# Loading the K and V caches of both batch entries as one unit of 4 MB

## The chip, the cores and the metric

One core of one Trainium2 chip runs the kernel; the other cores are idle. The metric is the device time of one execution in microseconds (us). PE is the matrix engine (TensorE), DVE is VectorE, ACT is ScalarE, POOL is GpSimd, and SyncE issues nearly all loads (77.66 of the 77.90 MB of packets are on its queue); a load writes into the 128 partitions (rows) of the on-chip memory. Ratios in this document are the mean time of one kernel's fast runs over that of the other's of the same rounds, so they are not quite the ratio of the medians that are quoted.

## The reference

It is one decoding step of attention over a cached window beside a dense layer, for two batch entries with one new token each:

```python
xn = layernorm(x)                                   # x is [2, 1, 448]
# A: 16 query heads, 8 key heads, Dh = 256; the last W = 4096 of 32768 cached positions
q = xn @ wq
p = softmax(q . k_cache[:, :, -4096:, :] / 16)
a = (p . v_cache[:, :, -4096:, :]) @ wo
# B: dense layer with a mish activation, 448 -> 1792 -> 448
h = xn @ w1 + b1
b = (h * tanh(softplus(h))) @ w2
out = x + a + b                                     # [2, 1, 448]
```

What matters is the amount of data: K and V are 2 entries x 8 heads x 4096 positions x 256 x 2 bytes each, 67.1 MB together. wq, wo, w1 and w2 add 10.6 MB. The compute is small.

The check of results is loose for this reference: softmax over 4096 nearly equal scores averages V to almost nothing, so the kernels below that mix up rows on purpose were also reported correct.

## The kernel before

Sixteen units (8 key heads x 2 entries), each with a 2 MB load of K and one of V. A load puts 32 positions (16 KB of contiguous memory) on each of the 128 partitions:

```python
def load_k(i):
    kvh, b = heads[i]
    t = k_pool.tile([P, T * Dh], BF16, tag="k", name="k")        # 4 buffers
    nc.sync.dma_start(
        out=t[:], in_=A_k_cache[b, kvh, s0:Sk, :].rearrange("(p t) d -> p (t d)", p=P)
    )
# load_v: the same from A_v_cache, 5 buffers; the last V comes in two halves
# load_wo: 448 KB for each key head
# ...
load_k(0); load_dense(); load_k(1)      # load_dense: w1 and w2
for i in range(NK + KA):
    # load_k(i + 2), load_v(i), load_wo
    # for each half: turn (DVE transposes K), scores (PE, ACT), turn_p (DVE transposes p)
    if i == 1:
        dense_out()                     # 28 products with w2
    if i >= KA:
        values(i - KA)                  # 64 products with V
        # mix: 8 products with wo, after every second unit
```

The softmax here doesn't subtract the row's maximum and nothing guards it: scores larger than these inputs give would overflow.

Of the kernel before, what the change touches and what calls it, by code (L numbers as in the profile page):

```python
# [9 lines left out]
ALU = mybir.AluOpType  # L10
AXIS = mybir.AxisListType
BF16 = mybir.dt.bfloat16
# [22 lines left out]
def kernel(  # L35
# [25 lines left out]
    F = B_w1.shape[1]  # L61
    T = W // P
    NH = 2
    TH = T // NH
    NX = 2
# [7 lines left out]
    NE = 2  # L73
    assert Sq == 1 and D * NX == NS * P and NS % 2 == 1 and HF % P == 0 and Hq % NX == 0
    assert TH * Q <= 512 and NB * NE * Q == Dh and ND == 2
# [3 lines left out]
    wo_pool = ctx.enter_context(tc.tile_pool(name="wo", bufs=3))  # L79
    k_pool = ctx.enter_context(tc.tile_pool(name="kk", bufs=4))  # L80
    v_pool = ctx.enter_context(tc.tile_pool(name="vv", bufs=5))
    kt_pool = ctx.enter_context(tc.tile_pool(name="kt", bufs=3))
# [14 lines left out]

    def v_tile(n):
        t = v_pool.tile([P, T * Dh], BF16, tag="v", name="v")
        return t[:, 0:n]  # L100



    SC = NS // 2 + 1
    wq_in = A_wq.rearrange("r (x n) -> (r x) n", x=NX).rearrange("(p s) n -> p s n", s=NS)
    wq_sb = []
    for lo, hi in ((0, SC), (SC, NS)):
        w = v_tile((hi - lo) * HW).rearrange("p (s n) -> p s n", n=HW)
        nc.sync.dma_start(out=w, in_=wq_in[:, lo:hi, :])  # L109
        wq_sb += [w[:, s, :] for s in range(hi - lo)]  # L110

# [35 lines left out]
    for b4 in range(NB):  # L147
        rows = slice(b4 * Q, (b4 + 1) * Q)
        for j in range(NQ):
            nc.vector.tensor_copy(  # L150
                out=spread[rows, b4, j * Q : (j + 1) * Q], in_=ident[rows, rows]
            )
    hsel = consts.tile([P, rep], FP32)
    nc.vector.tensor_copy(out=hsel[:], in_=ident[:, 0:rep])
    for j in range(1, NQ):
        nc.vector.tensor_tensor(
            out=hsel[:], in0=hsel[:], in1=ident[:, j * Q : j * Q + rep], op=ALU.add
        )
    NW = 3
    qdiag = []  # L160
# [46 lines left out]
    qrep = consts.tile([P, NB, HH, NE, NX, Bsz], BF16)  # L207
    wq_v = [w.rearrange("p (h m e) -> p h e m", h=HH, e=NE) for w in wq_sb]

    def project():  # L210
        qT_ps = ps_m.tile([P, HH, NE, NX * Bsz], FP32, tag="m", name="qT_ps")
        for hh in range(HH):
            for e in range(NE):
                for s in range(NS):
                    nc.tensor.matmul(  # L215
                        qT_ps[:, hh, e, :],
                        lhsT=wq_v[s][:, hh, e, :],
                        rhs=xs[:, s, :, :].rearrange("p x b -> p (x b)"),
                        start=(s == 0),
                        stop=(s == NS - 1),  # L220
                    )
# [11 lines left out]

    heads = [(kvh, b) for kvh in range(Hkv) for b in range(Bsz)]

    def build_q(i):
        kvh, b = heads[i]
        x, h0 = divmod(kvh * rep, HH)
        t = qdiag[i % NW]
        tv = t[:].rearrange("p (n e) c -> p n e c", e=NE)  # L240
        for j in range(NQ):
            rows = slice(j * Q, (j + 1) * Q)
            for e in range(NE):
                nc.gpsimd.tensor_copy(  # L244
                    out=tv[rows, :, e, j * Q : j * Q + rep],
                    in_=qrep[rows, :, h0 : h0 + rep, e, x, b],
                )
# [4 lines left out]

    def load_dense():
        dense["w1"] = v_tile(NS * HF).rearrange("p (s n) -> p s n", s=NS)
        nc.sync.dma_start(
            out=dense["w1"],
            in_=B_w1.rearrange("r (x n) -> (r x) n", x=NX).rearrange("(p s) n -> p s n", s=NS),
        )
        dense["w2"] = v_tile(NX * NF * D).rearrange("p (x c d) -> p x c d", x=NX, c=NF)
        nc.sync.dma_start(  # L260
            out=dense["w2"], in_=B_w2.rearrange("(x q c) d -> q x c d", x=NX, q=P)
        )

# [40 lines left out]
    def dense_out():  # L304
        w2_sb = dense.pop("w2")
        for x in range(NX):
            for c in range(NF):
                for n in range(NO):
                    add(
                        n,  # L310
                        act_bf[:, c, x, :],
                        w2_sb[:, x, c, n * DO : (n + 1) * DO],
                        start=False,
                        stop=False,
                    )


    NSTEP = len(heads) * NH
    k_t, kt_t, v_t, p_t, pT_t, wo_t = {}, {}, {}, {}, {}, {}
    state = {}  # L320

    def load_k(i):
        kvh, b = heads[i]
        t = k_pool.tile([P, T * Dh], BF16, tag="k", name="k")
        nc.sync.dma_start(  # L325
            out=t[:], in_=A_k_cache[b, kvh, s0:Sk, :].rearrange("(p t) d -> p (t d)", p=P)
        )
        k_t[i] = t

    def load_v(i, parts=1):  # L330
        kvh, b = heads[i]
        t = v_tile(T * Dh).rearrange("p (t d) -> p t d", t=T)
        vin = A_v_cache[b, kvh, s0:Sk, :].rearrange("(p t) d -> p t d", p=P)
        for u in range(parts):
            ts = slice(u * T // parts, (u + 1) * T // parts)
            nc.sync.dma_start(out=t[:, ts, :], in_=vin[:, ts, :])  # L336
        v_t[i] = t

    def load_wo(kvh, parts=1):
        w = wo_pool.tile([P, rep, ND * D], BF16, tag="wo", name="wo")  # L340
        r0 = kvh * rep * Dh
        win = A_wo[r0 : r0 + rep * Dh, :].rearrange("(h p c) d -> p h (c d)", h=rep, p=P)
        for u in range(parts):
            hs = slice(u * rep // parts, (u + 1) * rep // parts)
            nc.sync.dma_start(out=w[:, hs, :], in_=win[:, hs, :])
        wo_t[kvh] = w
# [11 lines left out]
    def scores(s):  # L358
# [13 lines left out]
        if s % NH == 0:  # L372
# [4 lines left out]
            func=ACT.Exp,  # L377
            scale=scale,
            accum_out=state["rs", i][:, s % NH : s % NH + 1],
        )  # L380
        p_t[s] = p_sb

    def turn_p(s):
        pT = p_pool.tile([P, TH * Q], BF16, tag="pT", name="pT", bufs=7)
        nc.vector.transpose(out=pT[:], in_=p_t.pop(s)[:])  # L385
# [4 lines left out]
        rs = state.pop(("rs", i))  # L390
        den = ps_den.tile([P, rep], FP32, tag="den", name="den")
        for n in range(NH):
            nc.tensor.matmul(  # L393
                den[:],
                lhsT=rs[:, n : n + 1].to_broadcast([P, P]),
                rhs=hsel[:],
                start=(n == 0),
                stop=(n == NH - 1),
            )
        state["rec", i] = small.tile([P, rep], FP32, tag="rec", name="rec", bufs=4)  # L400
        nc.vector.reciprocal(out=state["rec", i][:], in_=den[:])  # L401

    def values(i):
        kvh, b = heads[i]
        po = ps_o.tile([P, ND, rep], FP32, tag="o", name="o")
        vv = v_t.pop(i).rearrange("p t (m c) -> p t c m", c=ND)
        for t in range(T):
            half, th = divmod(t, TH)
            pTv = pT_t[i * NH + half][:].rearrange("p (t c) -> p t c", t=TH)
            for c in range(ND):  # L410
                nc.tensor.matmul(  # L411
                    po[:, c, :],
                    lhsT=vv[:, t, c, :],
                    rhs=pTv[:, th, 0:rep],
                    start=(t == 0 and c == 0),
                    stop=(t == T - 1),
                    skip_group_check=True,
                )
        if b == 0:
            state["oT"] = small.tile([P, ND, rep, Bsz], BF16, tag="oT", name="oT")  # L420
        oT = state["oT"]
        nc.vector.tensor_tensor(  # L422
            out=oT[:, :, :, b],
            in0=po[:],
            in1=state.pop(("rec", i))[:].unsqueeze(1).to_broadcast([P, ND, rep]),
            op=ALU.mult,
        )

    def mix(kvh):
        oT = state["oT"]  # L430
        w = wo_t.pop(kvh)
        for h in range(rep):
            for n in range(NO):
                for c in range(ND):
# [4 lines left out]
                        start=False,  # L439
                        stop=(kvh == Hkv - 1 and h == rep - 1 and c == ND - 1),  # L440
                    )

    NK = len(heads)
    KA = 2

    load_k(0)
    load_dense()
    load_k(1)
    project()
    build_q(0)  # L450
    build_q(1)
    turn(0)
    for i in range(NK + KA):
        if i + 2 < NK:
            load_k(i + 2)
        if i < NK:
            load_v(i, parts=1 if i < NK - 1 else 2)
            kvh, b = heads[i]
            if b == Bsz - 1:
                load_wo(kvh, parts=1 if i < NK - 1 else 2)  # L460
            for half in range(NH):
                s = i * NH + half
                if s + 1 < NSTEP:
                    turn(s + 1)
                scores(s)
                if s >= 1:
                    turn_p(s - 1)
            if i + 2 < NK:
                build_q(i + 2)
        if i == NK:  # L470
            turn_p(NSTEP - 1)
        if i == 0:
            dense_in()
        if i == 1:
            dense_out()
        if i >= KA:
            values(i - KA)
            kvh, b = heads[i - KA]
            if b == Bsz - 1:
                mix(kvh)  # L480

# [35 lines left out]
```

## Time and profile before

| | kernel before |
|---|---|
| median time | 194.66 us (194.61 to 194.78, 4 runs) |
| span in the profile | 192.7 us |
| read | 77.67 MB, mean 403 GB/s |
| PE busy, DVE busy | 130.4 us, 102.2 us |
| a 16 KB packet of K or V | mean 620 ns, median 613 ns |

The prediction shows the page's lines. To read them: the DMA row gives the mean busy share of the core's sixteen DMA engines in tenths, in 40 equal slices of the span. A 9 in nearly all slices says that the sixteen are full, so time is bytes over rate (77.67 MB at 403 GB/s are the 192.7 us of the span). In the trace each packet is one run of contiguous bytes, or one completion mark of a load: the 7652 packets on the SyncE queue of the kernel before are 6914 runs and 738 marks, sixteen marks for each load of 128 rows and two for the store of 2 rows. The number of marks of a load is taken as the number of engines that it ran on.

### The profile page before, as it was taken

To read this page: it belongs to the slowest core of one execution; us is meant where nothing else is said; L and a number is where in the kernel's file an instruction comes from. 1 tells how busy PE (TensorE), PEld (TensorE's weight loads), DVE (VectorE), ACT (ScalarE), POOL (GpSimd) and SP (SyncE) were. 2 spreads that over 40 slices of the span, in tenths; PEclk is the share of its full clock that TensorE was granted. 3 is DMA by queue.
4 is the path that set the end of the run, shared out by engine and by line. 5 is a ranking of instruction groups with operands and counts; after the bars stand their busy time and mean duration, and the time that the engine had idled before them with its cause. 6 is when DMAs were issued, how large, how long until landed. Compare 5 with 4: busy or idle time off the path is not lost.

```text
span 192.7 us, 3810 instructions
## 1 busy us (share of the span) xinstructions
PE 130.4 (68%) x1624; PEld 81.3 (42%) x1624; DVE 102.2 (53%) x137; ACT 25.5 (13%) x69; POOL 24.8 (13%) x138
## 2 busy tenths in 40 slices
PE   0242993999827985499709881797449592898854
PEld 0142381466513654246504651364324452364752
DVE  4605506996638390929264753838091744748101
ACT  5000110112200211012200220021101110021100
POOL 7004320022110112002200210020200200000000
PEclk9999996699995799669975998599957979589965
DMA  6999999999999999999999999999999999999960
GB/s 211 424 447 408 427 427 435 428 435 402 431 422 428 425 415 428 435 418 414 429 425 432 420 416 430 428 425 411 428 432 428 403 434 422 432 414 429 410 253 2
DMA packets 7674, 77.90 MB, mean 404 GB/s; under 512 B 741, under 2 KB 2793, under 8 KB 3050
## 3 DMA queue, kind: packets, MB, share of 16 engines
q1 hardware_dynamic: 7652, 77.66, 96.1%
q8 instruction: 12, 0.20, 0.4%
q14 instruction: 4, 0.03, 0.0%
q10 hardware_dynamic: 6, 0.01, 0.0%
HBM read 77.67 MB, written 0.00 MB: 403 GB/s over the span
## 4 chain that ended last, share of the span: by engine, by line
DMA 96%; PE 1%; SPq 1%; issue 0%; ACT 0%; DVE 0%
DMA v<-in_A_v_cache_dram 51%; DMA k<-in_A_k_cache_dram 18%; DMA wo<-in_A_wo_dram 17%; DMA v<-in_B_w_dram 10%; PE psA L201 1%; PE o L411 1%; SPq L109 0%; SPq L325 0%; ACT res L484 0%; DVE oT L422 0%; SPq L336 0%
## 5 line engine op out<-in xcount | busy, mean ns | idle before, releaser
L352 DVE STREAM_TRANSPOSE kt<-k 128x2048 f32<-128x2048 f32 x32 | 73.5, 2300 | 48.9 <-DMA k<-in_A_k_cache_dram 48.9
L364 PE MATMUL sc<-kt,qdiag 128*128 128x512 bf16 x256 | 75.0, 443 | 14.4 <-DVE kt L352 14.3
L364 PEld LDWEIGHTS <-qdiag 128*128 128x128 bf16 x256 | 26.1, 111 | 50.5 <-issue 24.1
L374 ACT ACTIVATE p<-sc 128x512 bf16<-128x512 f32 x32 | 19.1, 597 | 144.8 <-PE sc L364 140.9
L244 POOL COPY qdiag<-qrep 32x8 bf16<-32x8 bf16 x128 | 21.0, 186 | 125.3 <-PE sc L364 109.8
L201 PE MATMUL psA<-wo,oT 128*2 128x224 bf16 x64 | 12.5, 370 | 31.3 <-DVE oT L422 31.3
L411 PEld LDWEIGHTS <-v 128*128 128x128 bf16 x1024 | 27.9, 97 | 6.3 <-DMA v<-in_A_v_cache_dram 3.0
L411 PE MATMUL o<-pT,v 128*128 128x2 bf16 x1024 | 28.1, 163 | 2.7 <-DMA v<-in_A_v_cache_dram 2.7
L385 DVE STREAM_TRANSPOSE pT<-p 128x512 bf16<-128x512 bf16 x32 | 21.4, 671 | 0.0
L201 PEld LDWEIGHTS <-oT 128*2 128x2 bf16 x64 | 6.5, 111 | 34.6 <-DVE oT L422 32.0
L393 PEld LDWEIGHTS den<-hsel,rs 128*128 128x128 f32 x64 | 11.7, 227 | 3.8 <-issue 2.1
L401 DVE RECIPROCAL rec<-den 128x2 f32<-128x2 f32 x16 | 2.5, 153 | 18.7 <-PE den L393 18.7
L393 PE MATMUL den<-hsel,rs 128*128 128x2 f32 x64 | 9.4, 252 | 0.0
L215 PE MATMUL qT_ps<-xs,v 128*128 128x4 bf16 x112 | 3.3, 166 | 6.1 <-DMA v<-in_A_wq_dram 6.1
L422 DVE TENSOR_TENSOR oT<-o,rec 128x4 bf16<-128x4 f32 x16 | 2.1, 134 | 8.5 <-PE o L411 8.5
L374 ACT ACTIVATION_READ_ACCUMULATOR p<-sc 128x1 f32 x32 | 6.2, 194 | 0.0
L215 PEld LDWEIGHTS <-v 128*128 128x128 bf16 x112 | 3.1, 104 | 6.6 <-DMA v<-in_A_wq_dram 6.6
L224 DVE CAST qT<-qT_ps 128x64 bf16<-128x64 f32 x1 | 0.2, 225 | 7.0 <-PE qT_ps L215 7.0
L169 PE MATMUL xnT_ps<-ident,xn_bf 2*128 2x2 bf16 x7 | 0.5, 166 | 5.0 <-DVE xn_bf L133 5.0
L270 PE MATMUL hT_ps<-xs,v 128*128 128x4 bf16 x49 | 3.7, 195 | 0.0
L270 PEld LDWEIGHTS <-v 128*128 128x128 bf16 x49 | 3.2, 149 | 0.3
L201 PE MATMUL psA<-v,act_bf 128*2 128x224 bf16 x28 | 2.8, 259 | 0.0
(40 smaller groups left out, 22.5 us busy)
## 6 DMA issues: line engine op xcount, KB each, us to landing
k<-in_A_k_cache_dram SPq DMA_DIRECT2D x16, 2048.0 KB, 32.5
v<-in_A_v_cache_dram SPq DMA_DIRECT2D x15, 2048.0 KB, 34.8
v<-in_B_w_dram SPq DMA_DIRECT2D x2, 1568.0 KB, 21.2
wo<-in_A_wo_dram SPq DMA_DIRECT2D x7, 448.0 KB, 31.8
v<-in_A_wq_dram SPq DMA_DIRECT2D x1, 2048.0 KB, 7.8
v<-in_A_v_cache_dram SPq DMA_DIRECT2D x2, 1024.0 KB, 29.9
v<-in_A_wq_dram SPq DMA_DIRECT2D x1, 1536.0 KB, 11.1
wo<-in_A_wo_dram SPq DMA_DIRECT2D x2, 224.0 KB, 24.1
```

The costliest lines, as they stand in the source:

```text
L201: nc.tensor.matmul(psA[n][:, :], lhsT=lhsT, rhs=rhs, skip_group_check=True, **flags)
L215: nc.tensor.matmul(qT_ps[:, hh, e, :], lhsT=wq_v[s][:, hh, e, :], rhs=xs[:, s, :, :].rearrange("p x b -> p (x b)"), start=(s == 0), stop=( ...
L244: nc.gpsimd.tensor_copy(out=tv[rows, :, e, j * Q : j * Q + rep], in_=qrep[rows, :, h0 : h0 + rep, e, x, b],)
L270: nc.tensor.matmul(hT_ps[:, c, :, :].rearrange("p x b -> p (x b)"), lhsT=w1_v[:, s, c, :], rhs=xs[:, s, :, :].rearrange("p x b -> p (x b)" ...
L352: nc.vector.transpose(out=kt[:].bitcast(FP32), in_=k[:, half * TH * Dh : (half + 1) * TH * Dh].bitcast(FP32),)
L364: nc.tensor.matmul(psc[:], lhsT=qdiag[i % NW][:, n * NE + e, :], rhs=ktv[:, n, e, :, :], start=(n == 0 and e == 0), stop=(n == NB - 1 and ...
L374: nc.scalar.activation(out=p_sb[:], in_=psc[:].rearrange("p t c -> p (t c)"), func=ACT.Exp, scale=scale, accum_out=state["rs", i][:, s % N ...
L385: nc.vector.transpose(out=pT[:], in_=p_t.pop(s)[:])
L393: nc.tensor.matmul(den[:], lhsT=rs[:, n : n + 1].to_broadcast([P, P]), rhs=hsel[:], start=(n == 0), stop=(n == NH - 1),)
L401: nc.vector.reciprocal(out=state["rec", i][:], in_=den[:])
L411: nc.tensor.matmul(po[:, c, :], lhsT=vv[:, t, c, :], rhs=pTv[:, th, 0:rep], start=(t == 0 and c == 0), stop=(t == T - 1), skip_group_check ...
L422: nc.vector.tensor_tensor(out=oT[:, :, :, b], in0=po[:], in1=state.pop(("rec", i))[:].unsqueeze(1).to_broadcast([P, ND, rep]), op=ALU.mult,)
```

## The change

The intent: a unit is now one key head of both entries. Entry 0 lies on partitions 0 to 63 and entry 1 on 64 to 127, each partition holds 64 positions (32 KB in one run), and a load is 4 MB. The score products mix both entries' queries, and a bias of -10000 on the exponential masks the rows that hold no query of the entry. Of K and V there are two buffers each. w2 moves to the end of the loads, in three parts, with its 28 products behind everything else. The diff, cut:

```diff
-    T = W // P
-    NH = 2
-    TH = T // NH
+    PB = P // Bsz
+    T = W // PB
+    TH = 16
+    NH = T // TH
...
-    k_pool = ctx.enter_context(tc.tile_pool(name="kk", bufs=4))
-    v_pool = ctx.enter_context(tc.tile_pool(name="vv", bufs=5))
+    k_pool = ctx.enter_context(tc.tile_pool(name="kk", bufs=2))
+    v_pool = ctx.enter_context(tc.tile_pool(name="vv", bufs=2))
...
+    W2 = ((0, 0, NF), (1, 0, NF - 2), (1, NF - 2, NF))
+    def load_w2():
+        t = k_tile()[:, 0 : NX * NF * D].rearrange("p (x c d) -> p x c d", x=NX, c=NF)
...
-    def load_k(i):
-        kvh, b = heads[i]
-        t = k_pool.tile([P, T * Dh], BF16, tag="k", name="k")
-        nc.sync.dma_start(
-            out=t[:], in_=A_k_cache[b, kvh, s0:Sk, :].rearrange("(p t) d -> p (t d)", p=P)
-        )
+    def load_cache(t, cache, i, parts):
+        for u in range(parts):
+            ts = slice(u * T // parts * Dh, (u + 1) * T // parts * Dh)
+            src = cache[:, i, s0:Sk, :].rearrange("b (p t) d -> b p (t d)", p=PB)[:, :, ts]
+            nc.sync.dma_start(out=t[:, ts], in_=src)
...
             func=ACT.Exp,
             scale=scale,
+            bias=off[:],
...
+        if i == Hkv - 1:
+            load_w2()
...
+    dense_out()
```

More of the change, by code (lines that the diff above doesn't have):

```diff
@@ L61 @@
     F = B_w1.shape[1]
-    T = W // P
-    NH = 2
-    TH = T // NH
+    PB = P // Bsz
+    T = W // PB
+    TH = 16
+    NH = T // TH
+    BR = Bsz * rep
     NX = 2
@@ L73 @@
     NE = 2
-    assert Sq == 1 and D * NX == NS * P and NS % 2 == 1 and HF % P == 0 and Hq % NX == 0
+    assert Sq == 1 and PB % Q == 0 and D * NX == NS * P and NS % 2 == 1 and HF % P == 0 and Hq % NX == 0
     assert TH * Q <= 512 and NB * NE * Q == Dh and ND == 2
@@ L95, with k_tile, v_tile @@
     nc.scalar.dma_start(out=b1_sb[:, :], in_=B_b1.rearrange("(o f) -> o f", o=1))
-    def v_tile(n):
-        t = v_pool.tile([P, T * Dh], BF16, tag="v", name="v")
-        return t[:, 0:n]
-    SC = NS // 2 + 1
-    wq_in = A_wq.rearrange("r (x n) -> (r x) n", x=NX).rearrange("(p s) n -> p s n", s=NS)
-    wq_sb = []
-    for lo, hi in ((0, SC), (SC, NS)):
-        w = v_tile((hi - lo) * HW).rearrange("p (s n) -> p s n", n=HW)
-        nc.sync.dma_start(out=w, in_=wq_in[:, lo:hi, :])
-        wq_sb += [w[:, s, :] for s in range(hi - lo)]
+    def k_tile():
+        return k_pool.tile([P, T * Dh], BF16, tag="k", name="k")
+    def v_tile():
+        return v_pool.tile([P, T * Dh], BF16, tag="v", name="v")
+    wq_sb = v_tile()[:, 0 : NS * HW].rearrange("p (s n) -> p s n", s=NS)
+    nc.sync.dma_start(
+        out=wq_sb,
+        in_=A_wq.rearrange("r (x n) -> (r x) n", x=NX).rearrange("(p s) n -> p s n", s=NS),
+    )
     ident = consts.tile([P, P], BF16)
@@ L152 @@
             )
-    hsel = consts.tile([P, rep], FP32)
-    nc.vector.tensor_copy(out=hsel[:], in_=ident[:, 0:rep])
-    for j in range(1, NQ):
-        nc.vector.tensor_tensor(
-            out=hsel[:], in0=hsel[:], in1=ident[:, j * Q : j * Q + rep], op=ALU.add
-        )
-    NW = 3
+    hsel = consts.tile([P, Bsz, rep], FP32)
+    id_all = ident[:, :]
+    for u in range(PB // Q):
+        mine = bass.AP(
+            id_all.tensor,
+            id_all.offset + u * Q,
+            [list(id_all.ap[0]), [PB + rep, Bsz], [1, rep]],
+        )
+        if u == 0:
+            nc.vector.tensor_copy(out=hsel[:], in_=mine)
+        else:
+            nc.vector.tensor_tensor(out=hsel[:], in0=hsel[:], in1=mine, op=ALU.add)
+    off = consts.tile([P, 1], FP32)
+    nc.vector.tensor_reduce(out=off[:], in_=hsel[:], axis=AXIS.XY, op=ALU.add)
+    nc.vector.tensor_scalar(
+        out=off[:], in0=off[:], scalar1=1e4, scalar2=1e4, op0=ALU.mult, op1=ALU.subtract
+    )
+    NW = 2
     qdiag = []
@@ L207 @@
     qrep = consts.tile([P, NB, HH, NE, NX, Bsz], BF16)
-    wq_v = [w.rearrange("p (h m e) -> p h e m", h=HH, e=NE) for w in wq_sb]
+    wq_v = wq_sb.rearrange("p s (h m e) -> p s h e m", h=HH, e=NE)
     def project():
@@ L216, in project @@
                         qT_ps[:, hh, e, :],
-                        lhsT=wq_v[s][:, hh, e, :],
+                        lhsT=wq_v[:, s, hh, e, :],
                         rhs=xs[:, s, :, :].rearrange("p x b -> p (x b)"),
@@ L232, in project @@
         )
-    heads = [(kvh, b) for kvh in range(Hkv) for b in range(Bsz)]
     def build_q(i):
-        kvh, b = heads[i]
-        x, h0 = divmod(kvh * rep, HH)
+        x, h0 = divmod(i * rep, HH)
         t = qdiag[i % NW]
@@ L241, in build_q @@
         for j in range(NQ):
+            b = j * Q // PB
             rows = slice(j * Q, (j + 1) * Q)
+            cols = slice(j * Q + b * rep, j * Q + (b + 1) * rep)
             for e in range(NE):
                 nc.gpsimd.tensor_copy(
-                    out=tv[rows, :, e, j * Q : j * Q + rep],
+                    out=tv[rows, :, e, cols],
                     in_=qrep[rows, :, h0 : h0 + rep, e, x, b],
@@ L251, with load_w1 @@
     dense = {}
-    def load_dense():
-        dense["w1"] = v_tile(NS * HF).rearrange("p (s n) -> p s n", s=NS)
+    def load_w1():
+        dense["w1"] = v_tile()[:, 0 : NS * HF].rearrange("p (s n) -> p s n", s=NS)
         nc.sync.dma_start(
@@ L258, in load_dense @@
         )
-        dense["w2"] = v_tile(NX * NF * D).rearrange("p (x c d) -> p x c d", x=NX, c=NF)
-        nc.sync.dma_start(
-            out=dense["w2"], in_=B_w2.rearrange("(x q c) d -> q x c d", x=NX, q=P)
-        )
+    W2 = ((0, 0, NF), (1, 0, NF - 2), (1, NF - 2, NF))
+    def load_w2():
+        t = k_tile()[:, 0 : NX * NF * D].rearrange("p (x c d) -> p x c d", x=NX, c=NF)
+        w2_in = B_w2.rearrange("(x q c) d -> q x c d", x=NX, q=P)
+        for x, lo, hi in W2:
+            nc.sync.dma_start(out=t[:, x, lo:hi, :], in_=w2_in[:, x, lo:hi, :])
+        dense["w2"] = t
     def dense_in():
@@ L305, in dense_out @@
         w2_sb = dense.pop("w2")
-        for x in range(NX):
-            for c in range(NF):
-                for n in range(NO):
+        for x, lo, hi in W2:
+            for n in range(NO):
+                for c in range(lo, hi):
                     add(
@@ L313, in dense_out, with load_k, load_wo @@
                         start=False,
-                        stop=False,
+                        stop=(x == NX - 1 and c == NF - 1),
                     )
-    NSTEP = len(heads) * NH
+    NSTEP = Hkv * NH
     k_t, kt_t, v_t, p_t, pT_t, wo_t = {}, {}, {}, {}, {}, {}
     state = {}
-    def load_k(i):
-        kvh, b = heads[i]
-        t = k_pool.tile([P, T * Dh], BF16, tag="k", name="k")
-        nc.sync.dma_start(
-            out=t[:], in_=A_k_cache[b, kvh, s0:Sk, :].rearrange("(p t) d -> p (t d)", p=P)
-        )
-        k_t[i] = t
-    def load_v(i, parts=1):
-        kvh, b = heads[i]
-        t = v_tile(T * Dh).rearrange("p (t d) -> p t d", t=T)
-        vin = A_v_cache[b, kvh, s0:Sk, :].rearrange("(p t) d -> p t d", p=P)
-        for u in range(parts):
-            ts = slice(u * T // parts, (u + 1) * T // parts)
-            nc.sync.dma_start(out=t[:, ts, :], in_=vin[:, ts, :])
-        v_t[i] = t
-    def load_wo(kvh, parts=1):
+    def load_cache(t, cache, i, parts):
[3 more added lines that the diff above has]
+            nc.sync.dma_start(out=t[:, ts], in_=src)
+    def load_k(i, parts=1):
+        k_t[i] = k_tile()
+        load_cache(k_t[i], A_k_cache, i, parts)
+    def load_v(i, parts=1):
+        v_t[i] = v_tile()
+        load_cache(v_t[i], A_v_cache, i, parts)
+    def load_wo(kvh):
         w = wo_pool.tile([P, rep, ND * D], BF16, tag="wo", name="wo")
@@ L342, in load_wo @@
         win = A_wo[r0 : r0 + rep * Dh, :].rearrange("(h p c) d -> p h (c d)", h=rep, p=P)
-        for u in range(parts):
-            hs = slice(u * rep // parts, (u + 1) * rep // parts)
-            nc.sync.dma_start(out=w[:, hs, :], in_=win[:, hs, :])
+        nc.sync.dma_start(out=w[:], in_=win)
         wo_t[kvh] = w
@@ L383, in turn_p @@
     def turn_p(s):
-        pT = p_pool.tile([P, TH * Q], BF16, tag="pT", name="pT", bufs=7)
+        pT = p_pool.tile([P, TH * Q], BF16, tag="pT", name="pT", bufs=2 * NH + 1)
         nc.vector.transpose(out=pT[:], in_=p_t.pop(s)[:])
@@ L390, in turn_p @@
         rs = state.pop(("rs", i))
-        den = ps_den.tile([P, rep], FP32, tag="den", name="den")
+        den = ps_den.tile([P, BR], FP32, tag="den", name="den")
         for n in range(NH):
@@ L395, in turn_p @@
                 lhsT=rs[:, n : n + 1].to_broadcast([P, P]),
-                rhs=hsel[:],
+                rhs=hsel[:].rearrange("p b h -> p (b h)"),
                 start=(n == 0),
@@ L399, in turn_p @@
             )
-        state["rec", i] = small.tile([P, rep], FP32, tag="rec", name="rec", bufs=4)
+        state["rec", i] = small.tile([P, BR], FP32, tag="rec", name="rec")
         nc.vector.reciprocal(out=state["rec", i][:], in_=den[:])
     def values(i):
-        kvh, b = heads[i]
-        po = ps_o.tile([P, ND, rep], FP32, tag="o", name="o")
-        vv = v_t.pop(i).rearrange("p t (m c) -> p t c m", c=ND)
+        po = ps_o.tile([P, ND, BR], FP32, tag="o", name="o")
+        vv = v_t.pop(i)[:].rearrange("p (t m c) -> p t c m", t=T, c=ND)
         for t in range(T):
-            half, th = divmod(t, TH)
-            pTv = pT_t[i * NH + half][:].rearrange("p (t c) -> p t c", t=TH)
+            piece, th = divmod(t, TH)
+            pTv = pT_t[i * NH + piece][:].rearrange("p (t c) -> p t c", t=TH)
             for c in range(ND):
@@ L413, in values @@
                     lhsT=vv[:, t, c, :],
-                    rhs=pTv[:, th, 0:rep],
+                    rhs=pTv[:, th, 0:BR],
                     start=(t == 0 and c == 0),
@@ L418, in values @@
                 )
-        if b == 0:
-            state["oT"] = small.tile([P, ND, rep, Bsz], BF16, tag="oT", name="oT")
-        oT = state["oT"]
+        oT = small.tile([P, ND, rep, Bsz], BF16, tag="oT", name="oT")
         nc.vector.tensor_tensor(
-            out=oT[:, :, :, b],
-            in0=po[:],
-            in1=state.pop(("rec", i))[:].unsqueeze(1).to_broadcast([P, ND, rep]),
+            out=oT[:].rearrange("p c h b -> p c b h"),
+            in0=po[:].rearrange("p c (b h) -> p c b h", b=Bsz),
+            in1=state.pop(("rec", i))[:]
+            .rearrange("p (b h) -> p b h", b=Bsz)
+            .unsqueeze(1)
+            .to_broadcast([P, ND, Bsz, rep]),
             op=ALU.mult,
         )
+        state["oT", i] = oT
     def mix(kvh):
-        oT = state["oT"]
+        oT = state.pop(("oT", kvh))
         w = wo_t.pop(kvh)
@@ L439, in mix @@
                         start=False,
-                        stop=(kvh == Hkv - 1 and h == rep - 1 and c == ND - 1),
+                        stop=False,
                     )
-    NK = len(heads)
-    KA = 2
     load_k(0)
-    load_dense()
-    load_k(1)
+    load_w1()
     project()
@@ L452 @@
     turn(0)
-    for i in range(NK + KA):
-        if i + 2 < NK:
-            load_k(i + 2)
-        if i < NK:
-            load_v(i, parts=1 if i < NK - 1 else 2)
-            kvh, b = heads[i]
-            if b == Bsz - 1:
-                load_wo(kvh, parts=1 if i < NK - 1 else 2)
-            for half in range(NH):
-                s = i * NH + half
+    for i in range(Hkv + 1):
+        if i + 1 < Hkv:
+            load_k(i + 1)
+        if i < Hkv:
+            load_v(i, parts=1 if i < Hkv - 1 else 2)
+            load_wo(i)
+        if i == Hkv - 1:
+            load_w2()
+        if i < Hkv:
+            for piece in range(NH):
+                s = i * NH + piece
                 if s + 1 < NSTEP:
@@ L467 @@
                     turn_p(s - 1)
-            if i + 2 < NK:
+            if i + 2 < Hkv:
                 build_q(i + 2)
-        if i == NK:
+        else:
             turn_p(NSTEP - 1)
@@ L473 @@
             dense_in()
-        if i == 1:
-            dense_out()
-        if i >= KA:
-            values(i - KA)
-            kvh, b = heads[i - KA]
-            if b == Bsz - 1:
-                mix(kvh)
+        if i >= 1:
+            values(i - 1)
+            mix(i - 1)
+    dense_out()
     res = consts.tile([Bsz, D], BF16)
```

## The prediction

> **What bounds the kernel now.** I read the busy table first. No engine is full: PE 68% of the span, DVE 53%. Then the slices.
>
> ```profile
> span 192.7 us, 3810 instructions
> ...
> PE 130.4 (68%) x1624; PEld 81.3 (42%) x1624; DVE 102.2 (53%) x137; ACT 25.5 (13%) x69; POOL 24.8 (13%) x138
> ...
> DMA  6999999999999999999999999999999999999960
> GB/s 211 424 447 408 427 427 435 428 435 402 431 422 428 425 415 428 435 418 414 429 425 432 420 416 430 428 425 411 428 432 428 403 434 422 432 414 429 410 253 2
> ```
>
> The reader is to see that from the second slice to the 38th (4.8 us each) the sixteen DMA engines are over 90% busy and move 400 to 447 GB/s, without a gap. The chain that ended last says the same: transfers hold it, and only its last pieces are compute.
>
> ```profile
> DMA 96%; PE 1%; SPq 1%; issue 0%; ACT 0%; DVE 0%
> ```
>
> Its last pieces in order of time (start, us, what):
>
> ```profile
> 156.59 30.62 DMA v<-in_A_v_cache_dram
> 187.21 0.05 issue
> 187.26 1.02 PE o L411 x32
> 188.28 0.02 issue
> 188.31 0.18 DVE oT L422
> 188.48 0.04 issue
> 188.53 1.67 PE psA L201 x8
> ```
>
> The last data land at 187.2; 5.5 us of tail follow: the last 32 value products, the normalising multiply, eight output products, two copies, the store. The view by windows confirms the steady rate (stretch, us, busy time of PE, PEld, DVE, ACT, POOL, then granted clock, DMA share, GB/s):
>
> ```profile
> 60.00:80.00 20.00, 14.01 (x174) 8.40 (x173) 11.00 (x13) 2.75 (x8) 2.64 (x16) 0.84 1.01 425
> ...
> 120.00:140.00 20.00, 14.25 (x176) 8.55 (x176) 10.94 (x13) 2.75 (x8) 2.64 (x16) 0.84 1.01 424
> ```
>
> DMA share 1.01 (full) beside PE busy 14 of 20 us. So this is a stream of 77.66 MB through sixteen engines, 424/16 = 26.5 GB/s each, and everything else lies under it. The waits say so too: DVE's transposes waited 48.9 us in all for K loads. The question is thus only what the change does to the loads.
>
> The queue counts carry the step on which this prediction rests:
>
> ```profile
> q1 hardware_dynamic: 7652, 77.66, 96.1%
> ...
> q10 hardware_dynamic: 6, 0.01, 0.0%
> ```
>
> Queue 1 is the SyncE queue, with 46 loads of 128 rows and the 2-row store. Its runs of contiguous data are 2048 (K) + 2176 (V) + 256 (wq) + 128 (w1) + 256 (w2) + 2048 (wo) + 2 (out) = 6914 packets. 7652 - 6914 = 738 = 46 x 16 + 2: each 128-row load posted sixteen completion packets, the 2-row store two. Queue 10 is the ScalarE queue: x is two rows, b1 one run; 2 + 1 data packets and 2 + 1 completions are its 6. So a transfer of 128 rows runs on sixteen engines here, and one whose outermost count is 2 on two.
>
> [...]
>
> **The change part by part.** The intent: loads twice as large, half as many packets, a shorter tail.
>
> Compute: nearly equal work. The score products stay 256 of 512 columns (32 steps of 8), the value products 1024 (now of 4 columns instead of 2), the transposes 32 of K at 2300 ns and 32 of p at 671 ns. GpSimd's copies into qdiag halve from 128 to 64. The mask is a bias operand of the same 32 exponentials. Under a full queue none of this is worth anything.
>
> Packet overhead, if all engines were used: the single packet records of the trace have a median of 613 ns for 16 KB and 74 ns for 1792 B. The slope is (613 - 74)/(16384 - 1792) = 0.0369 ns a byte (27.1 GB/s), the rest 8 ns a packet. K and V in 32 KB runs have 128 packets fewer on each engine: 128 x 8 ns = 1.0 us. Sixteen loads fewer at 9 ns for the completion packet: 0.1 us. That is the whole gain from larger runs.
>
> The tail: w2 comes last, so that behind its last piece only 4 products remain; the value products, the multiply and the mix (1.0 + 0.2 + 1.7 us above) go under the transfer of w2 (1.6 MB, some 3.8 us at 425 GB/s). Dense-out's earlier 24 products may be late by a microsecond; I count 2 us off the tail.
>
> Engines: the built program shows the deciding thing. A load of K or V was source [128 rows][8192], destination [128][8192]. It is now source [2 batch entries, 134 MB apart][64 rows][16384 elements], destination [128 partitions][1][16384]. The two entries can't fold into one dimension of 128, because the batch stride isn't 64 rows. [...] So [...] fourteen engines get none of the 67.1 MB of K and V. The other loads (wq, w1, wo, w2) keep a source of 128 rows and stay on sixteen.
>
> Work of engine 0 then, with the durations above: K and V, 16 loads x 64 packets of 32 KB at 8 + 32768 x 0.0369 = 1217 ns: 1246 us (V's last load in two halves adds 64 x 8 ns = 0.5 us). wq 8 packets of 28,672 B: 8.5 us; w1 8 of 12,544 B: 3.8 us (8 x 470 ns); wo 8 loads x 16 packets x 74 ns: 9.5 us; w2 8 x (239 + 173 + 74 ns): 3.9 us; completions 30 x 9 ns: 0.3 us. Sum 1272.5 us.
>
> Does the queue run dry between? No. There are two buffers each for K and V, and a load takes 78 us on two engines, while the work on a K tile is 4 x 2.3 us of transposes with 4 x 0.7 us for p, and values of a tile 128 products, about 3.5 us by the 1.74 us for 64 in the timeline. When K of head i-1 lands, V of i-2 and K of i are queued behind it[...]; buffers come free some 12 us after a landing, with 78 to 156 us of work still queued.
>
> The end: transfers start near 2.1 us (the chain), so the last lands near 1275 us. Tail about 4 us (four products and some late ones 1.3, two copies 0.7, the store 2.1). Span about 1279; the timed runs are 194.63 where the span is 192.7, so 1.9 more: **1281 us**, 6.6 times the kernel before.
>
> **The rivals.** First, all sixteen engines: [...] only the small gains remain: 194.6 - 1.1 - 2 = about 191.5 us, -1.6%, just within 2%. For it: it is what the author must have meant, and nothing in this trace has a two-dimensional source against 128 partitions. Against it: the instruction carries the two dimensions apart[...]. Chance about one in ten.
>
> Second, sixteen engines, with compute becoming the bound: a head now lands as 4 MB at once, so its first transpose waits longer, and the last heads' compute might stick out. DVE's 102 us and PE's 130 us over the 185 us of transfers speak against more than a few microseconds: 192 to 197 us.
>
> Third, two engines with another rate than I take. [...] 27.1 GB/s stands, as the slope of packet durations suggests. If the sixteen were held back by something shared [...], two alone could be faster: 5% would give 1220 us. If one engine can't hide the latency of the memory alone, slower; the 8 ns between packets in the full stream give no hint of that.
>
> Fourth, two engines, but dry spells because of two buffers: each one would cost the 12 us of compute behind a landing, at most 16 times: up to 190 us more. The order of issue above speaks against it.
>
> **Range and chances.** With two engines I expect 1255 to 1305; the rate of an engine is measured to about 1%, and tail and start are a few microseconds. I take 1250 to 1310 for 8 in 10, with one in ten kept for sixteen engines and the rest for a different rate. Chances: slower 0.89, same 0.07, faster 0.04.
>
> **What would show it.** The DMA row of the slices should fall to 1 (two of sixteen engines, 0.125) after a first slice that also carries wq and w1, with GB/s near 54; queue 1's completion packets should be 13 x 16 for the other loads but 2 for each K and V load: 17 x 2. So its packet count should be 2048 + 128 (K and V with V's last in halves) + 128 + 128 + 2048 + 384 + 2 data, and 13 x 16 + 17 x 2 + 2 completions: 5110 in all, against 5348 for sixteen engines. A K load should take over 77 us from issue to landing, more where it queues. The mean of PE and DVE busy time should stay near 130 and 102 us, at a tenth of the span. Wrong would be: a DMA row of 9 throughout (rival one), or a row of 1 with holes of 0 (rival four), or GB/s well off 54 (rival three).

A load of 128 rows posted sixteen marks, the 2-row store two. Both ends of that store have 2 rows, and no load of the kernel before had an outermost count of 2 against 128 partitions. That such a load runs on two engines too was the author's estimate, and the counts were one point against the first rival.

## The result and the profile after

The changed kernel takes 1293.03 us (1291.65 to 1294.29, 4 runs) beside 194.66 us: ratio 6.642, 95% interval 6.630 to 6.653. Executions over 1.5% slower than the fastest of the same kernel are left out of the means.

The same parts of the page of the changed kernel; a slice is now 32.3 us:

```profile
span 1291.9 us, 3666 instructions
...
PE 134.0 (10%) x1624; PEld 80.9 (6%) x1624; DVE 99.6 (8%) x121; ACT 28.3 (2%) x69; POOL 13.4 (1%) x73
...
DMA  4111111111111111111111111111111111111130
GB/s 191 54 54 55 54 65 55 65 56 54 54 55 54 55 57 63 54 54 55 64 53 55 53 55 65 54 55 53 54 67 54 53 53 55 64 54 55 54 104 37
...
q1 hardware_dynamic: 5110, 77.66, 14.7%
```

Three things are to be seen. The DMA row is 1 where it was 9, without a 0 until the last slice: a steady stream, at 54 GB/s, twice the 27.1 GB/s of one engine. PE and DVE are busy for as long as before (134 against 130 us, 100 against 102), so compute did not grow. And the packets on the SyncE queue are 5110, the very count worked out for two engines, with two marks for each K and V load (sixteen would have given 5348).

Who waits for whom, from the waits of the changed kernel (total, times, longest):

```profile
DVE kt L366 <- DMA k<-in_A_k_cache_dram: 1010.0, 8, 144.8
...
PE o L425 <- DMA v<-in_A_v_cache_dram: 508.1, 9, 62.8
```

DVE sits idle for 1010 us in front of eight K loads; before it was 48.9 us. The time went into the loads and nowhere else. (The chain of waits names 89% of this span "another core or an unknown queue": it has no landing for the loads on two engines, and the page gives no time from issue to landing for them either. So for such loads the table of waits is the view to read.)

### The profile page after: what moved, and what is told of

Its sections match the earlier page's. It is cut to its first block, busy times and chain, and to the rows that moved or that the text cites. A ratio compares the mean times of both kernels' runs of the same rounds, so it can differ in the third digit from the quotient of the medians.

```text
span 1291.9 us, 3666 instructions
## 1 busy us (share of the span) xinstructions
PE 134.0 (10%) x1624; PEld 80.9 (6%) x1624; DVE 99.6 (8%) x121; ACT 28.3 (2%) x69; POOL 13.4 (1%) x73
## 3 DMA queue, kind: packets, MB, share of 16 engines
q1 hardware_dynamic: 5110, 77.66, 14.7%
## 4 chain that ended last, share of the span: by engine, by line
another core or an unknown queue 89%; PE 5%; DVE 4%; issue 1%; DMA 1%; ACT 0%; DVEq 0%
DVE kt L366 3%; PE sc L378 2%; PE psA L216 1%; DVE pT L400 1%; DMA v<-in_A_wq_dram 1%; PE den L408 1%; PE o L425 1%; PE qT_ps L230 0%; DVE rec L416 0%; ACT p L388 0%; DVE oT L434 0%; DVE qrep L245 0%; PE qr_ps L242 0%; DVEq L366 0%
## 5 line engine op out<-in xcount | busy, mean ns | idle before, releaser
L378 PE MATMUL sc<-kt,qdiag 128*128 128x512 bf16 x256 | 72.4, 434 | 157.6 <-DVE kt L366 157.6
L425 PE MATMUL o<-pT,v 128*128 128x4 bf16 x1024 | 28.8, 166 | 508.1 <-DMA v<-in_A_v_cache_dram 508.1
L388 ACT ACTIVATE p<-sc,off 128x512 bf16<-128x512 f32 x32 | 22.0, 687 | 1031.4 <-PE sc L378 1030.5
L258 POOL COPY qdiag<-qrep 32x8 bf16<-32x8 bf16 x64 | 10.5, 185 | 809.0 <-PE sc L378 794.3
L408 PEld LDWEIGHTS den<-hsel,rs 128*128 128x128 f32 x64 | 10.2, 228 | 1.9 <-issue 0.9
L408 PE MATMUL den<-hsel,rs 128*128 128x4 f32 x64 | 9.3, 269 | 0.0
L388 ACT ACTIVATION_READ_ACCUMULATOR p<-sc,off 128x1 f32 x32 | 6.2, 193 | 0.0
L216 PE MATMUL psA<-k,act_bf 128*2 128x224 bf16 x28 | 4.2, 329 | 0.0
L216 PEld LDWEIGHTS <-act_bf 128*2 128x2 bf16 x28 | 3.1, 109 | 1.1
```

What stands on the lines that cost most here:

```text
L216: nc.tensor.matmul(psA[n][:, :], lhsT=lhsT, rhs=rhs, skip_group_check=True, **flags)
L258: nc.gpsimd.tensor_copy(out=tv[rows, :, e, cols], in_=qrep[rows, :, h0 : h0 + rep, e, x, b],)
L378: nc.tensor.matmul(psc[:], lhsT=qdiag[i % NW][:, n * NE + e, :], rhs=ktv[:, n, e, :, :], start=(n == 0 and e == 0), stop=(n == NB - 1 and ...
L388: nc.scalar.activation(out=p_sb[:], in_=psc[:].rearrange("p t c -> p (t c)"), func=ACT.Exp, scale=scale, bias=off[:], accum_out=state["rs" ...
L408: nc.tensor.matmul(den[:], lhsT=rs[:, n : n + 1].to_broadcast([P, P]), rhs=hsel[:].rearrange("p b h -> p (b h)"), start=(n == 0), stop=(n ...
L425: nc.tensor.matmul(po[:, c, :], lhsT=vv[:, t, c, :], rhs=pTv[:, th, 0:BR], start=(t == 0 and c == 0), stop=(t == T - 1), skip_group_check= ...
```

## The experiments

Each is an edit of the changed kernel unless it says otherwise. "Theory A" is the prediction's: the outermost count of the source sets the number of engines. "Theory P" adds that it matters which partitions the engines write at the same time: in an unfavourable choice each gets half its rate. Its grounds, and statements of which engine writes which partitions, were not shown by any run. Its figures stand as estimates from the runs: packets near 2400 ns are twice the median of 1213 ns, four engines at half rate take the 1290 us of two, eight the 660 us or so that theory A gives for four, and 215 GB/s is half of what the kernel before moves in its full slices (400 to 447).

### One line: rows outermost, entries inside

```diff
-            src = cache[:, i, s0:Sk, :].rearrange("b (p t) d -> b p (t d)", p=PB)[:, :, ts]
+            src = cache[:, i, s0:Sk, :].rearrange("b (p t) d -> p b (t d)", p=PB)[:, :, ts]
```

> The changed kernel with only the order of the source dimensions of each K and V load turned: 64 rows outermost, the two batch entries inside (wrong result on purpose: entries interleave over the partitions). Same bytes, same 32 KB runs, same number of loads, same buffers, same 134 MB between the entries. Theory A (the outermost source count sets the number of engines; now 64, so 16 engines): about 191 us, DMA row at 9 throughout, 5348 packets on queue 1. Rival B (runs of 32 KB, loads of 4 MB or only two buffers are slow by themselves): stays near 1290 us. Rival C (two entries 134 MB apart are slow to read): clearly over 200 us.

Measured: 197.24 us (197.04 to 199.38), 1.016 of the kernel before (1.010 to 1.022).

```profile
DMA  7999999999999999999999999999999999999700
...
q1 hardware_dynamic: 5348, 77.66, 93.8%
```

All sixteen engines are full again and the packets are 5348. Bytes, 32 KB runs, loads of 4 MB, two buffers and the distance between the entries are as in the kernel that took 1293 us. So rivals B and C fall: the order of two dimensions costs 1096 us. The larger runs save little: packets of 32 KB take 1221 ns on average here, two of 16 KB 2 x 620 in the kernel before. The run is also 6 us over its expectation of 191; the last two experiments look at that.

### Four and eight outer blocks

```diff
-            src = cache[:, i, s0:Sk, :].rearrange("b (p t) d -> b p (t d)", p=PB)[:, :, ts]
+            hg, b, part = i % 2, (i // 2) % 2, i // 4
+            r0 = s0 + part * 32 * T
+            src = cache[b, 4 * hg : 4 * hg + 4, r0 : r0 + 32 * T, :].rearrange(
+                "h (p t) d -> h p (t d)", p=32)[:, :, ts]
```

(for eight: all 8 heads, 16 rows each)

> The changed kernel with the source of each K and V load as 4 heads x 32 rows of one batch entry (wrong result on purpose), 4 MB in 32 KB runs as before. Theory A alone (4 engines, each at the 27.1 GB/s of the single packets): 623 us of K and V an engine + 26 of the other loads + about 16 of start, slow packets and tail: about 665 us; 12 completion packets... 17 loads x 4 = 68 completions in place of 34, so 5144 packets on queue 1. [...] about 1290 us in spite of twice the engines, with single 32 KB packets near 2400 ns. Rival B (nothing to do with engines): 1290 us with packets of 1213 ns.

> The same with 8 heads x 16 rows (wrong result on purpose). Theory A alone, 8 engines: 312 + 26 + 16 = about 354 us. [...] about 660 us, packets near 2400 ns. Packets on queue 1 in both cases: 5076 + 17 x 8 = 5212. Rival B: 1290 us.

Measured: 750.78 us with four blocks, 632.2 us with eight (one run each). The figures, 1290 and 660 us, are those of theory P. The counts of packets are those of four and eight engines, 5144 and 5212 (four and eight marks a load), so theory A sets the number. But the number alone does not set the time: it would have been 665 and 354. Half the rate all the time (1290 us) does not fit the run with four blocks either; for eight it had given about 660. Eight engines took only 16% less time than four. The rate of the run with four blocks, from its page (a slice is 18.7 us):

```profile
DMA  9222322223222223222232223222322232222531
GB/s 284 52 58 59 89 65 65 70 74 95 82 96 96 109 100 119 102 110 108 110 115 110 105 110 122 108 109 107 127 107 110 108 121 113 105 110 103 162 117 46
```

Four engines are busy throughout (a 2 or 3 in the DMA row; a share of 0.26 to 0.28 in the windows), yet they begin at the 54 GB/s of two and reach the 108 GB/s of four only after some 300 us. Single 32 KB packets take a median of 1213 ns, but the slowest twentieth take 2472 ns or more, about twice as long. It would look like this if engines that hold each other up while in step came out of step in time; that is a reading, which no trace shows directly. The run with two engines below tests whether the destinations matter. With eight blocks the mean packet of the whole run takes 2314 ns.

### The right result on sixteen engines: one load for each entry

```diff
-            nc.sync.dma_start(out=t[:, ts], in_=src)
+            for b in range(Bsz):
+                src = cache[b, i, s0:Sk, :].rearrange("(p t) d -> p (t d)", p=PB)[:, ts]
+                nc.sync.dma_start(out=t[b * PB : (b + 1) * PB, ts], in_=src)
```

> The changed kernel with each K and V load issued as two loads, one for each batch entry: 64 rows to partitions 0 to 63, then 64 rows to partitions 64 to 127 (right result). The outermost counts are 64 and 64: 16 engines. Theory A alone: about 192 us. [...] 67.1 MB at about 215 GB/s is 312 us, with the other loads and the ends about 335 us, single 32 KB packets near 2400 ns. Rival B: well over 335 us.

Measured: 367.87 us (364.48 to 372.11; the slowest of the four runs is slow), 1.883 of before (1.874 to 1.893).

```profile
DMA  8999999999998999999999999999999999999991
GB/s 331 259 214 281 186 226 212 196 219 214 198 219 182 213 224 215 190 214 191 223 221 215 195 217 208 212 191 236 214 205 214 221 217 192 223 205 214 214 268 49
```

The DMA row looks like that of the kernel before, and the rate is half. Sixteen engines are "busy" (5620 packets: sixteen marks for each of the now twice as many loads) with packets of 2499 ns on average, where it was 1221 ns at the full rate. This fits theory P, though the time is 10% above its 335 us; A alone (192 us) falls as a theory of the time.

### Sixteen outer blocks, far and near

```diff
+            r0 = s0 + i * 8 * T                                       # far: 2 entries x 8 heads, 16.8 MB apart
+            src = cache[:, :, r0 : r0 + 8 * T, :].rearrange(
+                "b h (p t) d -> (b h) p (t d)", p=8)[:, :, ts]
...
+            src = cache[b, i, r0 : r0 + 16 * 9 * T, :].rearrange(     # near: 16 blocks of one head
+                "(q p t) d -> q p (t d)", q=16, p=9)[:, 0:8, ts]
```

> The changed kernel with the source of each K and V load as 16 outer blocks (2 entries x 8 heads, one even stride of 16.8 MB) of 8 rows (wrong result on purpose). 16 engines, 5348 packets on queue 1. Theory A alone: as with the rows outermost, about 197 us. [...] near the 368 us of the load split by entry, with packets up to 2400 ns; less if the engines drift apart, as in the run with four outer blocks, whose rate rose from 52 to 110 GB/s while it ran: 250 to 368 us.

> The run with 16 outer blocks (361 us) differs from the one with the rows outermost (197 us) in two ways: [...] the sixteen sources lie 16.8 MB apart, an even power of two. Here the 16 blocks of 8 rows come from one head, 295 KB apart (wrong result on purpose); partitions and engines as in the run with 16 outer blocks. Theory P (which partitions the engines write in step decides): about 361 us again, 32 KB packets near 2450 ns. Rival H (the far, even distance of the sources decides): about 197 us, packets near 1215 ns.

Measured: 360.69 us far, 361.95 us near, with 32 KB packets of 2478 ns on average in the near run (one run each). In the first expectation the figures behind the cut are those of theory P. The rows of the page of the near run:

```profile
DMA  8999999999999999999999999999999999999992
GB/s 329 265 220 291 193 215 215 198 222 217 197 222 185 219 227 211 204 216 213 209 218 222 205 220 207 215 190 236 217 215 213 215 204 220 207 215 207 215 249 94
```

The distance of the sources does nothing here (rival H falls; at half the rate a smaller effect could be hidden). What then differs from the run with the rows outermost (also sixteen engines and 5348 packets, 197 us)? Theory P says the partitions that the engines write at one time, but that is argued: the trace names neither the engine nor the partition of a packet. If each engine took one unbroken share of four rows there, it too would write eight partitions in a row (four rows of two entries) and should be slow. So for theory P to hold, the shares must lie otherwise in that run, and no run here shows how.

### Two engines, the two blocks of a load 32 partitions apart

```diff
-            nc.sync.dma_start(out=t[:, ts], in_=src)
+            for g in range(2):
+                nc.sync.dma_start(
+                    out=t[g * 64 : (g + 1) * 64, ts], in_=src[:, g * 32 : (g + 1) * 32, :])
```

> The changed kernel with each K and V load cut by row into two loads, whose outermost source count is still 2 (wrong result on purpose): the first takes 32 rows of each entry to partitions 0 to 63, the second to partitions 64 to 127. Two engines as before the cut, the same bytes and runs[...]. Theory P: [...] packets near 2430 ns at least at the start, 2500 us in all if they stay in step, less (down to 1300 us) if they drift apart as in the run with four blocks. Rival H or any theory in which only the number of engines counts: 1293 us, packets of 1213 ns from the start.

Measured: 1362.92 us (one run), and 5144 packets: 34 more completion marks, as the loads are twice as many. From the windows of this run (length, busy times, then granted clock, DMA share, GB/s):

```profile
20.00:60.00 40.00, 0.00 (x0) 0.00 (x0) 0.00 (x0) 0.00 (x0) 0.00 (x0) 1.00 0.12 29
60.00:100.00 40.00, 0.00 (x0) 0.00 (x0) 0.00 (x0) 0.00 (x0) 0.00 (x0) 1.00 0.13 33
100.00:140.00 40.00, 0.00 (x0) 0.00 (x0) 0.00 (x0) 0.00 (x0) 0.00 (x0) 1.00 0.13 35
140.00:200.00 60.00, 14.37 (x95) 8.18 (x94) 10.25 (x6) 3.12 (x8) 1.33 (x8) 0.65 0.15 47
200.00:400.00 200.00, 15.73 (x168) 8.94 (x168) 12.62 (x15) 3.35 (x9) 1.32 (x8) 0.52 0.13 55
```

The same view of the changed kernel:

```profile
20.00:100.00 80.00, 4.87 (x12) 1.71 (x12) 7.15 (x4) 0.78 (x2) 0.00 (x0) 1.00 0.13 54
```

The same number of engines (a share of 0.12 to 0.13 in the first 100 us), the same sources: in the changed kernel they ran at 54 GB/s in the window from 20 to 100 us. Here, where the program puts the two outer blocks of a load 32 partitions apart instead of 64, they begin at 29 GB/s, about the rate of one (27.1), and reach 55 GB/s after some 200 us. By the packet records a 32 KB packet takes 2195 ns on average from 20 to 60 us and 1219 ns from 220 to 300 us; that the two drift apart in between is the likely reading. The loads are halves, but size is not the cause, as the same loads reach 55 GB/s later in this run. What is left is the destination partitions as the program gives them. That each of the two engines takes one of the two blocks was the author's reading; the trace names no partitions. The other runs with 4, 8 and 16 blocks lose about half as well: four begin at 52 to 59 GB/s where 4 times the 27.1 GB/s of one engine would be 108, eight stay at 109 to 134 in the slices up to 500 us (217), sixteen near 215 throughout (434).

### Both halves from two queues

```diff
-            nc.sync.dma_start(out=t[:, ts], in_=src)
+            for b, eng in ((0, nc.sync), (1, nc.scalar)):
+                src = cache[b, i, s0:Sk, :].rearrange("(p t) d -> p (t d)", p=PB)[:, ts]
+                eng.dma_start(out=t[b * PB : (b + 1) * PB, ts], in_=src)
```

> As the load split by entry (right result), but entry 0 issued from SyncE and entry 1 from ScalarE[...]. Theory A alone: about 195 us. [...] in step it is again 368 us, fully out of step 195 us; I expect something between, about 240 us. It must be below 368 us by over 10% [...].

Measured: 359.04 us (353.84 to 363.34; two of the four runs are slow), 1.843 of before. The figures, 368 to 195 us, are theory P's. This expectation failed: the gain over one queue is 3.0% between the means of the fast runs (355.8 against 366.7 us), not over 10%. The expectation took it that every engine would have packets of both halves at the same time. The packet records don't show that: I looked every 10 us at which packets were in flight, and in many of these looks, above all in the first 100 us, all or nearly all were of one queue, hence one half. Over the run the 32 KB packets take 2313 ns on average (2499 with one queue); where the halves in flight were mixed, they still took about 2200 ns. So the run is no clean test. By the criterion that I had set it speaks against theory P; the run with two engines and blocks 32 apart speaks for it without this gap. What keeps the packets long on two queues stays open.

### The other loads out of the way

```diff
-        if i == Hkv - 1:
-            load_w2()
...
-    load_k(0)
     load_w1()
+    load_w2()
+    for i in range(Hkv):
+        load_wo(i)          # only head 0 loads, the others use its tile
+    load_k(0)
```

> The changed kernel with w1 and w2 loaded before the first K, and only one wo load, also before it, used for all heads (wrong result on purpose); K and V still on two engines. Where do the 12 us go that the prediction lacked? Theory: 32 KB packets of the two engines are slowed while other engines carry w1, wo or w2. Then all packets of K and V take about 1213 ns: 16 x 77.5 us = 1240, start 20.6, tail 10.2, launch 1.9: about 1273 us. Rival: slow packets come by themselves: about 1280 us.

Measured: 1274.29 us (1273.94 and 1274.65). K and V packets of 32 KB take 1214.9 ns on average, two of 1920 over 1300 ns; in the changed kernel the mean was 1224.2 ns. So the slow packets go with the other loads: 24 of the 32 packets over 1300 ns in the changed kernel overlap a packet of wq, w1 or wo in time. These loads use the two engines of K and V as well as the other fourteen (sixteen marks each in the count of 5110), and the run does not tell which of the two slows the packets. Part of the difference to 1293 us is simply the seven wo loads that are left out here (some 8 us by the prediction's 1.18 us each).

### The other part of the change alone, on the kernel before

```diff
+            if i == NK - 1:
+                load_w2()      # in three parts, into a K buffer
...
-        if i == 1:
-            dense_out()
...
+    dense_out()
```

> The kernel before (one entry per load, 16 KB runs) with only the other part of the change: w2 loaded last in three parts, its products at the end. My prediction took 2 us off for this. The run with the rows outermost says otherwise: there the 28 products of w2 took 4.95 us on the path after the last mix. If my tail estimate was right: 192.6 us. If the products of w2 behind the mix eat it: V's last half lands about 5 us earlier, then 1.0 + 0.2 + 1.7 us of values and mix and 4.2 to 5 us of w2 products: 194.5 to 195.5 us, no gain.

Measured: 195.01 us (194.58 to 195.52, 6 runs), ratio 1.0014 (0.9999 to 1.0029): no gain. The end of its timeline (start, length):

```profile
183.53 1.01 PE L417 MATMUL o<-pT,v 128*128 128x2 bf16 x32 [1.51 <-DMA v<-in_A_v_cache_dram]
...
184.58 0.17 DVE L428 TENSOR_TENSOR oT<-o,rec 128x4 bf16<-128x4 f32 x1 [4.08 <-PE o L417]
...
184.80 1.65 PE L201 MATMUL psA<-wo,oT 128*2 128x224 bf16 x8 [0.26 <-DVE oT L428]
...
186.69 4.40 PE L201 MATMUL psA<-k,act_bf 128*2 128x224 bf16 x28 [0.23 <-DMA k<-in_B_w_dram]
```

V's last half is there 3.7 us earlier than before (183.5 against 187.2), and the 28 products of w2 then take 4.4 us behind the mix (2.8 us in the second unit of the kernel before). The first of them still waited 0.23 us for w2. By the packet records the data of its three parts end at 186.1, 187.5 and 188.1 us: they come so late and so close together that hardly any of the products could have run before the mix ended at 186.5 us.

### Sixteen engines, with w2 early again

The run with the rows outermost, with w2 behind w1 and its products in the second unit:

```diff
+    load_w2()                  # behind load_w1()
...
+        if i == 1:
+            dense_out()
...
-    dense_out()
```

> The kernel of the run with the rows outermost (16 engines, 197.2 us, wrong result on purpose), but w2 loaded behind w1 as before the change and its products done early. What cost it 2.5 us against the kernel before: w2's products at the end, or the unit of one head of 4 MB? Theory W (w2's 28 products, 4.95 us, behind the last mix): V's last half then lands near 187.2, 64 products 1.9, multiply and mix 1.9, copies and store 2.8: span about 194, 195.5 us timed. Theory U (a late head's compute runs behind its landing, whatever is last): 197 us.

Measured: 197.7 us (196.38 to 198.43, 6 runs), 1.0147 of before (1.0114 to 1.0179). Theory W falls, U stands: also without w2 at the end this kernel is 1.5% behind the kernel before. The end of the chain of its last unit, with pieces left out:

```profile
170.13 3.29 PE sc L378 x8
...
179.47 1.91 PE sc L378 x8
181.37 3.19 PE o L425 x128
...
187.14 3.20 PE o L425 x114
...
190.58 1.67 PE psA L216 x8
```

K of the last head lands at 165.4 us, and from there transposes, scores, the values of the head before, its mix, and the values of the last head follow one another up to 192.3 us. In the kernel before, a unit is half as large and only 32 products and a mix are left after the last landing. Whether having two buffers each plays a part was not tested. This is the prediction's second rival, which it had put at 192 to 197 us; the 197.2 and 197.7 us lie just above. It was hidden in the changed kernel by the slow loads.

No version here beats the kernel before.

## Why the prediction was right

**Two engines.** Right, and the step that carried it: an estimate then, shown now. The packet count of 5110 was met exactly, the DMA row fell to 1, and one line that puts 64 rows outermost brings back 1096 us.

**No dry spells.** Right in its outcome: the stream has no gap. The reason differs in part. The prediction had the next loads queued behind the current one. In the trace the issue itself waits: SyncE's instruction for the first V load takes 72.45 us, and the one after it 74.03 us (0.43 us for the first K load of the kernel before).

```profile
7.71 11.76 SPq L345 DMA_DIRECT2D k<-in_A_k_cache_dram  x1
19.59 72.45 SPq L345 DMA_DIRECT2D v<-in_A_v_cache_dram  x1
92.08 74.03 SPq L359 DMA_DIRECT2D wo<-in_A_wo_dram  x1
```

**The sum.** 1281 us against 1293, too low by 12 us, inside the range. The term that was too small is the packets of K and V, taken at one duration for all. By the prediction's terms V's last half lands at 1269.4 us (2.1 + 8.5 + 1246.2 + 0.5 + 3.8, and seven wo loads at 1.18); it landed near 1281.6. From the packet records: 960 packets of 32 KB an engine at 1224.2 instead of 1217 ns are 6.9 us, 128 halves of the last V at 640.8 instead of 612.5 ns are 3.6 us, a later start of the first K and the wo packets about 1 us each. The run with the other loads out of the way shows what goes with the first: 1214.9 ns when nothing else runs. That the slope from 1792 B and 16 KB packets held for 32 KB to within 0.6% is the part that went well.

**The tail.** The step "four products and some late ones, 1.3 us" was wrong: all 28 products ran behind the last mix, 4.2 us in the changed kernel:

```profile
1281.67 1.87 PE L425 MATMUL o<-pT,v 128*128 128x4 bf16 x64 [39.78 <-DMA v<-in_A_v_cache_dram]
...
1283.80 1.65 PE L216 MATMUL psA<-wo,oT 128*2 128x224 bf16 x8 [0.26 <-DVE oT L434]
...
1285.24 4.19 PE L216 MATMUL psA<-k,act_bf 128*2 128x224 bf16 x28
```

From V's last landing the prediction's terms give about 9 us to the end and the profile 10.2, so it hardly showed in 1293. That is luck: the prediction counted the transfer of wo and w2 there (about 5 us), and the path in the trace is values, mix and all 28 products instead. But the 2 us that rival one took off for the tail did not exist, as the kernel before with w2 last shows.

**The rivals.** Rival one (all sixteen engines, 191.5 us) did not come, and would not have been 191.5 either: with sixteen engines the kernel takes 197.2. Rival two names the likely cause of that. Rival three (another rate for two engines alone): two engines kept the 27.1 GB/s of the slope in the changed kernel (54 GB/s from 20 to 100 us), where the two blocks of a load go to partitions 64 apart. The prediction had not asked for a condition on the destinations. With the two blocks 32 apart the rate began at 29 GB/s and the run took 1363 us.

## What to carry to other kernels

Count a load's packets before you believe its size: here the completion marks told how many engines it ran on, with 2, 4, 8 and 16 marks a load for outermost source counts of 2, 4, 8 and 16, and 16 for a count of 64. An outermost count of 2 left fourteen of sixteen idle in the loads of K and V, although their runs were 32 KB and each load 4 MB. When a busy row is full but the rate is half, compare single packet durations: here they took 2499 ns in place of 1221 in the load split by entry, and 2195 at the start of the run with two blocks 32 partitions apart, in place of 1219 later in that run. And the larger unit was not free even at full rate here, because the last unit's compute came after its landing.
